# Two extra PSUM banks of a first layer: two one-bank tiles instead of the halves of a two-bank tile

## The chip, the core and the metric

The kernel runs on one core of a Trainium2 chip. A core has a matrix engine (TensorE, PE in the profile; its weight loads are shown apart as PEld), three engines for element-wise work (VectorE or DVE, ScalarE or ACT, GpSimd or POOL) and SyncE (SP), which here issues DMAs. POOL issues DMAs too. The engines run side by side, each through its own instructions in order, and wait for one another through semaphores. A matmul writes into PSUM, a small memory that is cut into banks; one bank holds 128 x 512 numbers of 32 bits. VectorE and ScalarE read it from there.

The metric is the device time of one execution in microseconds (us). Less is better.

## What is computed

Attention with two kinds of fixed mask, followed by a two-layer network with a leaky activation:

```python
def _attn_ref(q, k, v):                      # [8, 8, 576, 64] each
    stride = 32
    scores = (1 / sqrt(64)) * q @ k^T
    rel = pos[:, None] - pos[None, :]
    mask_local = (rel >= 0) & (rel < stride)                       # heads 0 to 3
    mask_strided = (rel >= 0) & (pos[None, :] % stride == pos[:, None] % stride)   # heads 4 to 7
    scores = where(mask, scores, -1e9)
    return softmax(scores) @ v

def _moe_ref(x, w_in, w_out, alpha):         # x [4608, 512], w_in [512, 2048], w_out [2048, 512]
    h = x @ w_in
    g = maximum(h, 0) + alpha * minimum(h, 0)
    return g @ w_out                         # [4608, 512]

x = attention output with its heads side by side: [8 * 576, 512]
```

## The kernel before

**Tiling.** The 4608 tokens are nine chunks of 512. Layer 1 of a chunk is 16 groups m = 0 to 15 of 128 hidden features each; a group is four matmuls of 128x512 (one for each 128 of the 512 input features, kk) that add up in one PSUM bank. ScalarE then writes the negative part to SBUF (`neg`, L646), and VectorE joins it with the bank to the activated group `gT[:, m]` (the function `fin` in `lin1_piece`, L649). Only after `fin` may the bank be written again. Layer 2 of chunk 0 is 16 pieces ("M" 0 to 15, `lin2_piece`, L664): four token tiles of four pieces, each piece four matmuls that read four groups of `gT` and a quarter of `wout`.

Attention goes batch by batch, in pairs of heads: a pair g is number g % 4 of batch g // 4, and pairs 2 and 3 of a batch are strided. Its steps are T (transposes of q and k, L255, with the tails t of the last 64 tokens, L273 and L278), S (scores, ScalarE's exponential and a mask, L421 to L443 from batch 2 on), P (attention times v, `pv_piece`, L469, with VectorE's division L478 and L480) and X (transposes of the result to xT, L488). P waits for the mask of the scores it reads. T is named by u, half a batch: T 3 q is the strided half of batch 1, T 4 of batch 2 the other half.

**Order.** Everything is kept in program order on each engine. For batch 0 and chunk 0 that order is written out as a list (`first`): loads, casts, attention of batch 0, and at its end the marker "B" and the first matmuls of groups 2, 1 and 0 ("L"), of which layer 1's loop does the last kk. Then the loop `for m in (2, 1, 0, *range(3, 16))` runs layer 1 of chunk 0 with no attention in between (`attn_n(0, 0)` does none). A second list runs layer 2 of chunk 0 mixed with attention of batch 1: M 0, M 1, M 2, M 4, M 3, then T 3 q, M 5, t 3, T 3 k, and so on. From chunk 1 on, layer 1 and layer 2 pieces alternate with attention steps of later batches, which come from a list `pieces`; the attention functions there also issue casts and loads to POOL and transposing DMAs (`transpose_d`, L137) to SyncE. A piece of g = 8 issues to POOL, in this order: its first mask (L436), the two copies of the strided v of batch 2 (L195, from the loaded tile `stv`), the next v load (L175) and, when the deferred exponentials are done, its second mask (L443).

**PSUM.** There are eight banks in three pools. `pspool` (tag "ps") has three slots of one bank that are given out in turn: transposes (`tp`, `tt`), outputs of P (`pv`), of X (`xp`) and, from batch 2 on, half of the scores (`sph`) use them. `phpool` has three banks hb0 to hb2, each a tile of its own. `pbpool` has a single tile of two banks (tag "sp"), which the scores use.

`hbank` (L84) gives out banks for layer 1, layer 2 and some of the scores, from a list `banks`, in the order of the list `turn` of indices: it takes the first one and puts it at the end. Up to "B" only hb0 and hb1 turn (hb2 is the target of matmuls on zeros, L815, that occupy TensorE at the start). At "B" `more_banks` (L875) takes the two-bank tile from `pbpool`, appends its two halves to `banks` as numbers 3 and 4, and sets `turn` so that groups 2, 1, 0, 3, 4 get hb2, hb0, hb1, half 0, half 1, and so on in that circle of five: m = 3, 8 and 13 use half 0 and m = 4, 9 and 14 use half 1. After layer 1 the numbers 3 and 4 leave `turn`. The framework places the tiles and derives the waits between engines from which instruction uses which tile.

Of the kernel before, what the change touches and what calls it, by code (L numbers as in the profile page):

```python
# [9 lines left out]
F32 = mybir.dt.float32  # L10
# [21 lines left out]
def kernel(  # L32
# [13 lines left out]
    B, H, S, D = q.shape  # L46
# [16 lines left out]
    pspool = ctx.enter_context(tc.tile_pool(name="ps", bufs=3, space=bass.MemoryType.PSUM))  # L63
    phpool = ctx.enter_context(tc.tile_pool(name="ph", bufs=1, space=bass.MemoryType.PSUM))
    pbpool = ctx.enter_context(tc.tile_pool(name="pb", bufs=1, space=bass.MemoryType.PSUM))
# [15 lines left out]
    banks = [phpool.tile([128, 512], F32, tag=f"hb{i}", name=f"hb{i}") for i in range(3)]  # L81
    turn, busy = [0, 1], []
# [534 lines left out]
    def lin1_mm(n, m, kks, first, last):  # L617
        if first:
            hcur[m] = hbank()
        hps = hcur[m]  # L620
        c0 = (512 * n) % RING
        parts = [(c0, 0, min(512, RING - c0))]
        if c0 + 512 > RING:
            parts.append((0, RING - c0, 512 - (RING - c0)))
        for kk in kks:
            for x, (src, dst, w) in enumerate(parts):
                keep(nc.tensor.matmul(  # L627
                    hps[:, dst : dst + w],
                    win16[:, kk, 128 * m : 128 * m + 128],
                    xT[:, kk, src : src + w],  # L630
                    start=(first and kk == kks[0] and x == 0),
                    stop=(last and kk == kks[-1] and x == len(parts) - 1),
                    skip_group_check=True,
                ))
        return hps

    def lin1_piece(n, m):
        if n not in gTs:
            gTs[n] = gpool.tile([128, 16, 512], F16, tag="gT", name="gT")
        if n == 0 and m < 3:  # L640
            hps = lin1_mm(n, m, (0,), False, True)
        else:
            hps = lin1_mm(n, m, (2, 0, 3, 1) if n == 1 else range(4), True, True)

        neg = npool.tile([128, 512], F32, tag="neg", name="neg")
        keep(nc.scalar.activation(neg, hps, AF.Relu, scale=-1.0))  # L646

        def fin():
            keep(nc.vector.scalar_tensor_tensor(  # L649
                gTs[n][:, m, :], neg, oma[:, m : m + 1], hps, op0=ALU.mult, op1=ALU.add))  # L650
        late.append(fin)
# [168 lines left out]
    def load_unit(b, strided, v_too=True):  # L820
# [3 lines left out]
        if v_too:  # L824
# [7 lines left out]
            name=nc.get_next_instruction_name(), act_func_set_id=6, ins=[], outs=[]  # L832
# [39 lines left out]
        for c, second in which:  # L872
            load_w(c, second)

    def more_banks():  # L875

        sp = pbpool.tile([128, 2, 512], F32, tag="sp", name="sp")
        banks.extend([sp[:, 0], sp[:, 1]])
        turn.insert(0, 2)
        turn.extend([3, 4])  # L880

    do = {
        "T": lambda u, nm: transpose_piece(u, nm),
        "t": lambda u: tails(u // 2, u, u % 2 == 1),
# [7 lines left out]
        "A": slope,  # L892
        "W": warm,
        "L": lambda m, hp: lin1_mm(0, m, (hp,), hp == 2, False),
        "B": more_banks,
    }

    first = [
# [22 lines left out]
    def attn_n(n, end):  # L921
        for _ in range(n):
            attn_step(end)
        if n == 0:
            attn_step(0)

    for m in (2, 1, 0, *range(3, 16)):
        lin1_piece(0, m)
        attn_n(0, 0)
    for z in (3, 4):  # L930
# [88 lines left out]
```

## Time and profile before

| | |
|---|---|
| time, median of 4 runs | 308.64 us (308.52 to 308.95) |
| time of the profiled execution | 308.6 us |
| its span, first to last instruction | 306.7 us |
| mean granted TensorE clock | 0.994 |
| TensorE busy | 295.0 us (96%), 2775 matmuls |
| VectorE, ScalarE, POOL busy | 222.1, 176.7, 168.4 us |
| chain that ended last, by engine | PE 85%, DMA 4%, DVE 4%, POOL 3% |

The span in forty slices of 7.67 us, busy share in tenths, and the granted clock:

```
PE   7997789999999999999999999999999999999995
DVE  5785638968853889588857886788668958955872
ACT  3753527577556776477647764776477236516630
POOL 8862288539769873877397719771836102101300
PEclk9997999999999999999999999999999999999999
```

How to read it: a 9 is a slice that is busy for 90% or more. Layer 1 of chunk 0 lies in slices three to six (19.5 to 41.3 us), layer 2 of chunk 0 from there to 64 us. Matmuls are pipelined and their ends are modelled, so a following matmul starts up to 0.15 us before the shown end of the one before. An entry in square brackets behind a line of the timeline is the idle time of the engine before it and what ended it. Where an instruction waits for several things, the view names the one that came last by its own account.

### The profile page before, as it was taken

The numbers are of one execution on the slowest core, as the hardware profiler recorded it, in microseconds if no ns is written. First come the engines' busy times: TensorE is split into PE (matmuls) and PEld (weight loads), VectorE is DVE, ScalarE is ACT, GpSimd is POOL, SyncE is SP. The second block draws the span as 40 slices with busy tenths as digits, with TensorE's granted clock in tenths as the row PEclk, the third lists the DMA queues.
The fourth block names the chain that finished last, engine by engine and source line by source line (L and its number), as shares of the span: only waits on it lengthen the run. The fifth ranks groups of instructions, "written<-read, shape, count | busy, mean of one in ns | idle before, by whom it ended". The sixth has DMA issues, their size and how long they took to land.

```text
span 306.7 us, 7027 instructions
## 1 busy us (share of the span) xinstructions
PE 295.0 (96%) x2775; PEld 191.8 (63%) x2775; DVE 222.1 (72%) x421; ACT 176.7 (58%) x330; POOL 168.4 (55%) x178
## 2 busy tenths in 40 slices
PE   7997789999999999999999999999999999999995
PEld 3562345654555458845888888448844874685484
DVE  5785638968853889588857886788668958955872
ACT  3753527577556776477647764776477236516630
POOL 8862288539769873877397719771836102101300
PEclk9997999999999999999999999999999999999999
DMA  7999997999799981999389938972821040012004
GB/s 226 191 205 207 205 223 200 144 174 204 207 153 209 218 106 16 148 302 117 41 141 295 116 35 126 209 83 37 183 82 22 0 142 18 2 66 72 2 0 139
DMA packets 81201, 40.38 MB, mean 132 GB/s; under 512 B 58624, under 2 KB 76304, under 8 KB 81168
## 3 DMA queue, kind: packets, MB, share of 16 engines
q0 software_dynamic: 41728, 17.38, 48.5%
q1 hardware_dynamic: 39168, 22.03, 30.8%
q10 hardware_dynamic: 272, 0.52, 0.6%
q8 instruction: 22, 0.36, 0.5%
q14 instruction: 11, 0.09, 0.1%
HBM read 38.01 MB, written 9.44 MB: 155 GB/s over the span
## 4 chain that ended last, share of the span: by engine, by line
PE 85%; DMA 4%; DVE 4%; POOL 3%; ACT 1%; issue 1%; ACTq 0%; POOLq 0%
PE hb L627 39%; PE hb L757 25%; PE hb L664 7%; PE pv L469 4%; DMA tl<-in_q_dram 2%; DMA ql<-in_q_dram 2%; PE tp L255 2%; PE sp L421 2%; PE sp L627 2%; DVE gT L649 2%; PE opl L757 1%; DVE gsum L709 1%; PE sph L421 1%; PE xp L488 1%; ACT neg L646 1%
## 5 line engine op out<-in xcount | busy, mean ns | idle before, releaser
L627 PE MATMUL hb<-xT,win 128*128 128x512 f16 (+1 forms) x616 | 129.1, 360 | 0.0
L649 DVE SCALAR_TENSOR_TENSOR gT<-neg,oma,hb 128x512 f16<-128x512 f32 x138 | 100.8, 744 | 36.4 <-ACT neg L646 29.9
L646 ACT ACTIVATE neg<-hb 128x512 f32<-128x512 f32 x138 | 82.2, 597 | 37.3 <-PE hb L627 36.7
L627 PEld LDWEIGHTS <-win 128*128 128x128 f16 x640 | 60.1, 98 | 60.6 <-issue 8.2
L436 POOL TENSOR_TENSOR et<-et,consts 128x576 f16<-128x576 f16 (+1 forms) x24 | 30.6, 1277 | 43.5 <-ACT et L434 43.4
L709 POOL TENSOR_TENSOR gsum<-gT 128x512 f16<-128x512 f16 x21 | 24.1, 1149 | 52.0 <-DVE gT L649 52.0
L757 PEld LDWEIGHTS <-gsum 128*128 128x128 f16 x448 | 41.6, 98 | 4.9 <-DVE gsum L709 0.2
L480 DVE TENSOR_TENSOR x<-pv,rc 96x384 f16<-96x384 f32 (+2 forms) x62 | 33.0, 532 | 2.1
L757 PEld LDWEIGHTS <-gT 128*128 128x128 f16 x336 | 31.5, 98 | 4.8
L443 POOL TENSOR_TENSOR et<-et,consts 128x576 f16<-128x576 f16 (+1 forms) x24 | 31.5, 1314 | 2.2 <-ACT et L440 2.2
L664 PE MATMUL hb<-wout,gT 128*128 128x512 f16 x128 | 31.9, 379 | 0.2 <-ACT osb L669 0.2
L469 PEld LDWEIGHTS <-et 72*128 72x128 f16 (+1 forms) x448 | 23.8, 98 | 10.5 <-DVE x16s L480 0.6
L769 ACT COPY o<-hb 128x512 f32<-128x512 f32 (+1 forms) x28 | 15.8, 565 | 24.1 <-PE hb L757 24.1
L757 PE MATMUL hb<-wout,gT 128*128 128x256 f16 x216 | 27.3, 273 | 0.0
L757 PE MATMUL hb<-wout,gsum 128*128 128x256 f16 x216 | 26.9, 273 | 0.0
L434 ACT ACTIVATE et<-sp 128x576 f16<-128x576 f32 (+1 forms) x24 | 15.5, 645 | 18.3 <-PE sp L421 16.7
L757 PE MATMUL hb<-wsum,gsum 128*128 128x256 f16 x216 | 26.0, 273 | 0.0
L772 DVE TENSOR_TENSOR o<-hb,o 128x512 f32<-128x512 f32 (+1 forms) x21 | 14.3, 679 | 14.7 <-PE hb L757 10.7
L478 DVE RECIPROCAL rc<-pv 72x6 f32<-72x6 f32 (+2 forms) x80 | 14.6, 182 | 10.2 <-PE pv L469 9.9
L440 ACT ACTIVATE et<-sph 128x288 f16<-128x288 f32 (+1 forms) x48 | 18.9, 409 | 0.0
L664 PEld LDWEIGHTS <-gT 128*128 128x128 f16 x128 | 11.0, 97 | 9.8 <-issue 0.2
L469 PE MATMUL pv<-vs,et 72*128 72x65 f16 x256 | 15.6, 194 | 0.3 <-DVE x16s L480 0.3
(107 smaller groups left out, 330.6 us busy)
## 6 DMA issues: line engine op xcount, KB each, us to landing
out_dram<-o SPq DMA_DIRECT2D x27, 256.0 KB, 4.0
kl<-in_k_dram SPq DMA_DIRECT2D x6, 512.0 KB, 7.7
ql<-in_q_dram SPq DMA_DIRECT2D x5, 512.0 KB, 7.2
stv<-in_v_dram POOLq DMA_DIRECT2D x8, 288.0 KB, 7.3
vl<-in_v_dram POOLq DMA_DIRECT2D x6, 384.0 KB, 8.2
win<-in_moe_w_in_dram POOLq DMA_DIRECT2D x4, 512.0 KB, 12.6
wout<-in_moe_w_out_dram POOLq DMA_DIRECT2D x4, 512.0 KB, 16.6
out_dram<-osb SPq DMA_DIRECT2D x8, 256.0 KB, 4.5
```

The source lines that it names most:

```text
L436: keep(nc.gpsimd.tensor_tensor(mv, mv, m, op=ALU.mult))
L440: keep(nc.scalar.activation(ev[:, n * y : n * y + n], sps[y][0:r, 0:n], AF.Exp, scale=SCALE))
L443: keep(nc.gpsimd.tensor_tensor(mv, mv, m, op=ALU.mult))
L469: keep(nc.tensor.matmul(pv[:, 65 * x : 65 * x + 65], et[0:r, c : c + 128], v16[0:r, 2 * P.pr + hh, t, :] if P.strided else v16[:, 6 * (2 * ...
L480: keep(nc.vector.tensor_tensor(P.x16[0:w, c0 : c0 + 64 * nb].rearrange("r (c e) -> r c e", e=64), pvv[:, :, 0:64], rc[0:w, 0:nb].unsqueeze ...
L627: keep(nc.tensor.matmul(hps[:, dst : dst + w], win16[:, kk, 128 * m : 128 * m + 128], xT[:, kk, src : src + w], start=(first and kk == kks ...
L646: keep(nc.scalar.activation(neg, hps, AF.Relu, scale=-1.0))
L649: keep(nc.vector.scalar_tensor_tensor(gTs[n][:, m, :], neg, oma[:, m : m + 1], hps, op0=ALU.mult, op1=ALU.add))
L664: keep(nc.tensor.matmul(ops, gTs[n][:, kf, 128 * mt : 128 * mt + 128], wout16[:, kf, :], start=(kf == 0), stop=(kf == 15)))
L709: keep(eng.tensor_tensor(o[:, k0:k1], x[:, k0:k1], y[:, k0:k1], op=op))
L757: keep(nc.tensor.matmul(dst, lhs[:, kf, 128 * mt : 128 * mt + 128], rhs[:, kf, :], start=(first and own and kf == 0), stop=(kf == 7), skip ...
L769: keep(nc.scalar.copy(o, x))
```

## The change

`more_banks` and its two-bank tile go. The marker "B" now only puts hb2 at the head of `turn`. In the loop of layer 1, ahead of groups 3 and 4, one tile of one bank each is taken from `pspool`, appended to `banks` as number 3 or 4, and its number is put at the head of `turn`. The circle of five is the same as before. No instruction is added or removed, and the two tiles go back to their pool when their last reader (the `fin` of m = 13 and of m = 14) is done.

```diff
-    def more_banks():
-
-        sp = pbpool.tile([128, 2, 512], F32, tag="sp", name="sp")
-        banks.extend([sp[:, 0], sp[:, 1]])
-        turn.insert(0, 2)
-        turn.extend([3, 4])
-
...
-        "B": more_banks,
+        "B": lambda: turn.insert(0, 2),
...
     for m in (2, 1, 0, *range(3, 16)):
+        if m in (3, 4):
+            banks.append(pspool.tile([128, 512], F32, tag="ps", name="hx"))
+            turn.insert(0, m)
         lin1_piece(0, m)
         attn_n(0, 0)
```

## The prediction

> **What bounds the kernel now.** I read the page first: TensorE is busy 295.0 of 306.7 us, so a gain must come from where it is idle or slow. Its row of forty slices is below 9 in the first fifth alone, and the granted clock is below 9 only in the fourth slice (23.0 to 30.7 us). That is layer 1 of chunk 0. So I asked the trace for the line of those matmuls in all, L627, and then for TensorE in order of time.
>
> ```profile
> its engine sat idle before it (us, times) until:
>   issue: 8.2, 11
>   DVE gT L649: 5.1, 3
> ```
>
> Line L627 waits for VectorE three times in the whole run, 5.1 us together ("issue" is the weight loads, which wait for nothing that counts). The timeline (start, length, instructions) says where:
>
> ```profile
> 22.80 1.03 PE L627 MATMUL sp<-xT,win 128*128 128x512 f16 x4
> 25.97 1.26 PE L627 MATMUL sp<-xT,win 128*128 128x512 f16 x4 [2.15 <-DVE gT L649]
> 27.03 4.24 PE L627 MATMUL hb<-xT,win 128*128 128x512 f16 x12
> 31.11 1.03 PE L627 MATMUL sp<-xT,win 128*128 128x512 f16 x4
> 33.60 1.02 PE L627 MATMUL sp<-xT,win 128*128 128x512 f16 x4 [1.47 <-DVE gT L649]
> 34.46 2.75 PE L627 MATMUL hb<-xT,win 128*128 128x512 f16 x12
> 37.05 1.03 PE L627 MATMUL sp<-xT,win 128*128 128x512 f16 x4
> 39.55 1.02 PE L627 MATMUL sp<-xT,win 128*128 128x512 f16 x4 [1.47 <-DVE gT L649]
> ```
>
> Banks are used in the order hb2, hb0, hb1, sp half 0, sp half 1. The second half waits each time. For what, VectorE's timeline shows:
>
> ```profile
> 25.18 0.74 DVE L649 SCALAR_TENSOR_TENSOR gT<-neg,oma,sp 128x512 f16<-128x512 f32 x1
> ...
> 32.80 0.75 DVE L649 SCALAR_TENSOR_TENSOR gT<-neg,oma,sp 128x512 f16<-128x512 f32 x1
> ```
>
> The first ends at 25.92 and half 1 starts at 25.97; the second ends at 33.55 and half 1 starts at 33.60. So half 1 waits until half 0, written just before it, has been read. The two share no element. No hb bank waits for its neighbour: being one tile is what ties them.
>
> The first wait costs more than itself. Windows of line L627:
>
> ```profile
> core 0: us, PE busy (x) PEld busy (x), PEclk, DMA share, GB/s
> 26.50:27.10 0.60, 0.60 (x4) 0.20 (x2) 0.60 1.24 205
> 27.60:28.00 0.40, 0.40 (x3) 0.12 (x2) 0.50 1.25 207
> 30.00:30.50 0.50, 0.50 (x4) 0.24 (x3) 0.97 1.23 203
> ```
>
> The clock is 0.60, then 0.50, and back at 30.0.
>
> **The sum in this stage.** A matmul of 128x512 takes 0.216 us in a row without waits (the chain of waits has 12 in 2.59 us), a group of four 0.864. From m = 3 (22.80) to the first matmul of layer 2 (41.27) there are 13 groups: 13 x 0.864 = 11.23, but 18.47 pass. The excess is 7.24: waits of 2.15 + 1.47 + 1.47 = 5.09; 0.15 for each that the modelled end of the matmul before covers, 0.45; and the slow clock, 0.6 x 0.40 + 2.9 x 0.50 = 1.7.
>
> [...] In the trace the slow stretch follows the 2.15 us wait within 0.6 us and lasts 3.4; the two 1.47 us waits have none behind them. I take the trace: all **7.24 us** go, and a new wait of about 2 us can bring 1.7 back.
>
> **What takes their place.** The new tiles come from the pool of three one-bank slots that transposes and attention outputs use. The two slots that m = 3 and m = 4 get held the outputs of P(0,1) and X(1), which VectorE has read by 21.5; TensorE wants them at 22.80 and 23.66. Cost nothing. Both stay taken until VectorE has finished m = 13 and m = 14, while layer 2's first transposes (T 3 q) want slots. These come behind M 3, which needs m = 15 finished, so that too is covered; without that cover they would wait up to one 0.60 us ACT and one 0.75 us DVE instruction. The order of banks and the number of instructions do not change. Waits that only name another instruction: below, a tenth of a us either way; I take nothing.
>
> Can the next engine keep up? Per group ACT needs 0.60 and VectorE 0.75 us, under 0.864. VectorE starts its first at 23.20 and is behind by four; m = 5, 6 and 7 want banks at 24.5, 25.4 and 26.3, read by 23.9, 24.6 and 25.2. The weights: win's four loads were issued at 7.80, 9.75, 11.14, 11.9 and took 11.6, 12.1, 13.2, 15.0, so m = 4, 8 and 12 have theirs at 21.9, 24.4, 26.9 and want them at 23.7, 27.1, 30.6. Layer 2 would begin at 34.03.
>
> **Layer 2, 7.2 us early.** From 20 to 58 us POOL waits for landings and then works through its casts; it waits for TensorE only at 62.04. These times stay. Each item that TensorE needs from there, moved 7.24 early:
> - wout's last two quarters land at 34.5 and 37.1 (18.1 + 16.4, 18.8 + 18.2); M 2 and M 3 want them at 35.8 and 37.5. Nothing.
> - T 3 q stands at 45.59, so 38.35; qs lands at 19.7 + 18.7 = 38.4. A tenth.
> - t 3 stands at 46.99, so 39.75; its tail lands at 27.1 + 13.2 = 40.35. **The lead falls to about 6.5.**
> - T 2 q, t 2, T 2 k, P(4,0), T 4 q, T 4 k: at 43.4, 45.6, 46.7, 51.8, 53.6, 56.7 with lead 6.5; casts and loads are done at 42.8, 45.1, 45.4, 50.1, 51.2, 53.7. Nothing.
>
> **Chunk 1.** It starts at 57.5 instead of 64.08, and here POOL's order bites:
>
> ```profile
> 68.09 1.27 POOL L436 TENSOR_TENSOR et<-et,consts 128x576 f16<-128x576 f16 x1 [4.62 <-ACT et L434]
> 69.32 2.01 POOL L195 COPY vs<-stv 72x1024 f16<-72x1024 f16 x2
> 71.28 0.82 POOL L175 DMA_DIRECT2D stv<-in_v_dram  x1
> 72.12 1.29 POOL L443 TENSOR_TENSOR et<-et,consts 128x576 f16<-128x576 f16 x1
> ```
>
> The second mask ends at 73.41 and P(8,1), which reads it, starts on TensorE at 73.83. With the lead the first mask is at 61.6, but the copies read a load issued at 55.09 that took 9.5 us to land: 64.6. From there copies 2.0, DMA issue 0.8, mask 1.3: end 68.74. P(8,1) stood 0.4 behind its mask; of that I count 0.3 as room (the rest, an estimate, as the start after a release). TensorE waits from 67.3 to 68.8, **1.5 us**, and the lead is 73.41 - 68.74 + 0.3 = **5.0**.
>
> Does that load land at 64.6 again? SyncE's two transposes of q and k (issued 64.02 and 67.06, landed 6.7 and 6.3 later) sit behind the last store of layer 2, and would now start when their source lands, 53.6 + 6.9 = 60.5, beside the end of this load. The nearest rows: vl loads took 6.4 us without these transposes (issued 51.2) and 7.7 with them (62.0), so at most 1.3 later. [...] I take the rows, 0.4 between 0 and 1.3, since only the last part of the load meets them.
>
> Behind it: the k transpose lands near 63.6 + 6.3 = 69.9, wanted by the score at 75.86 - 4.6 = 71.3; the next k load (issue 71.33 + 7.3 = 78.6, where POOL's cast starts at 78.69) moves with the transposes, 3.4 us, and lets P(10,0), which has 2.1 us of slack, start 5.5 early. Neither is tighter than 4.6. From 64 us on TensorE is busy in every slice and waits 0.3 us in all, so the lead reaches the end.
>
> **Forecast: 7.2 - 0.7 - 1.5 - 0.4 = 4.6 us.** The profiled execution took 308.6 us (span 306.7, 1.9 around it), as the median 308.64: **304.0 us**. Its own range is 302.9 to 305.0.
>
> **Rivals.**
> - *The loads are early* (10%). A later v load (71.28) landed 5.8 us after issue. Then the copies wait for nothing, mask 2 ends at 66.9, and if the source of the transposes comes 1 us early too, P(10,0) lets the lead stand at 6.5: 302.1. With the v load alone P(10,0) would set 5.5, which is 303.1 and in the forecast's own range. Against: 9.5 is this very load, and nothing ahead of it changes.
> - *The clock falls again* (22%). The wait at P(8,1) reaches 2 us, and half rate takes 1.7 again: lead 2.6 to 3, 306.0. For: 1.5 plus the 0.4 is at the edge. Against: 1.47 did not do it.
> - *The lead is lost at 64 us* (4%). The chain of waits gives 6.92 us from 57.03 to a tail load that ends at the matmul at 63.97; if it held, the stage would end where it does: 308.6. Against: the tile read there is loaded at 45.3 and 45.9, landing 5.4 and 5.0 later; VectorE's copy that frees the slot ends at 63.7 and explains the wait.
> - *Slower* (7%). The v load is held up by the transposes beyond 14.5 us, past 69.6 us, where the lead is used up; with half rate behind so long a wait, past 67.9. Landing at 70.5 gives 308.6 + 0.9 + 1.7 = 311.2. For: loads issued at 20 to 22 took 18.7 and 17.5. Against: those stood behind the eight weight loads.
>
> The forecast has 56%. The range is 302.0 to 306.6: it takes in the first two rivals and leaves out the last two and the tails. 0.2%, 0.6 us, is what a measurement of this kernel tells from no change. Faster 0.89, within 0.04, slower 0.07.
>
> **What would show it.** No wait of line L627 for VectorE between 22 and 42 us, clock 1.00 there, layer 2 at 34.0; a wait of half a us at t 3; chunk 1 at 57.5; one wait of 1.5 to 2 us at P(8,1) near 67 us for POOL; none after. Wrong if the second new bank still waits for the first, if layer 2 stalls for loads beyond 1 us, or if the clock falls elsewhere.

## The result and the profile after

The changed kernel is no faster than the one before: ratio of times 1.0018 [0.9998, 1.0038], where the forecast of 304.0 us was 0.985. The ratio leaves out executions more than 1.5% above the fastest of the same kernel, which are 18 of 33 of the changed kernel and 3 of 54 of the kernel before; over all of them the medians are 310.98 us (305.86 to 315.13) and 307.85. No gain is to be seen in either count. The profiled execution took 309.59 us with a span of 307.8, against 308.6 and 306.7 before.

Up to 68 us the trace does what the sum said. TensorE's timeline of the changed kernel (start, length, engine, line, instructions; in brackets the idle time before and what ended it):

```profile
23.05 1.89 PE L627 MATMUL hx<-xT,win 128*128 128x512 f16 x8
24.77 2.75 PE L627 MATMUL hb<-xT,win 128*128 128x512 f16 x12
27.36 1.89 PE L627 MATMUL hx<-xT,win 128*128 128x512 f16 x8
...
33.41 1.03 PE L627 MATMUL hb<-xT,win 128*128 128x512 f16 x4
34.27 4.48 PE L664 MATMUL hb<-wout,gT 128*128 128x512 f16 x20
...
57.10 2.75 PE L627 MATMUL hb<-xT,win 128*128 128x512 f16 x12
...
68.77 0.36 PE L469 MATMUL pv<-vl,et 128*128 128x65 f16 x6 [1.75 <-POOL et L443]
68.96 1.89 PE L627 MATMUL hb<-xT,win 128*128 128x512 f16 x8
```

The two new banks (`hx`) are written in one go, eight matmuls without a wait. From m = 3 (23.05) to layer 2 (34.27) 11.22 us pass. Layer 2 begins 7.00 us early (41.27 before), chunk 1 6.98 early (64.08 before), and behind P(8,1)'s wait the lead is still 5.06 us (73.83 before). Then it is lost. The table of TensorE's waits (total us, times, longest) and the timeline go on:

```profile
PE sp L421 <- DMA kT<-ksd: 3.5, 1, 3.5
PE pv L469 <- POOL et L443: 1.8, 1, 1.8
```

```profile
74.40 0.42 PE L421 MATMUL sp<-qT,kT 64*128 64x72 f16 x8 [3.54 <-DMA kT<-ksd]
...
74.99 3.60 PE L627 MATMUL hb<-xT,win 128*128 128x512 f16 x8
...
81.16 1.89 PE L664 MATMUL hb<-wout,gT 128*128 128x512 f16 x8
```

The score S(10), the first that reads the q and k which SyncE transposes by DMA, waits 3.54 us for k. It started at 75.86 before, so 1.46 us of lead are left. Behind it eight matmuls take 3.60 us instead of 1.89, and layer 2 of chunk 1 begins 6.76 us after the score (74.40 to 81.16), where the kernel before needed 4.20 (75.86 to 80.06). That is 2.56 us more: 1.46 - 2.56 = -1.10, and the spans differ by just that. The windows show why (stretch, its length, busy us of PE, PEld, DVE, ACT and POOL with instructions, granted clock, DMA share, GB/s):

```profile
core 0: us, PE busy (x) PEld busy (x) DVE busy (x) ACT busy (x) POOL busy (x), PEclk, DMA share, GB/s
68.00:70.00 2.00, 1.23 (x11) 0.68 (x12) 1.17 (x3) 0.00 (x0) 2.00 (x3) 1.00 1.56 56
72.00:74.00 2.00, 0.00 (x0) 0.00 (x0) 0.27 (x1) 0.00 (x0) 0.00 (x0) 0.74 1.91 159
74.00:76.00 2.00, 1.60 (x19) 0.93 (x20) 0.00 (x0) 0.94 (x2) 0.00 (x0) 0.50 1.08 305
76.00:78.00 2.00, 2.00 (x7) 0.65 (x5) 0.45 (x1) 0.89 (x2) 1.04 (x1) 0.50 1.05 386
78.00:80.00 2.00, 2.00 (x12) 0.98 (x11) 1.04 (x3) 0.60 (x1) 2.00 (x2) 0.55 1.17 373
```

The clock falls to 0.50 during the wait and stays there until almost 80 us. In the row of forty slices the low clock has moved with it, from the fourth slice (layer 1 of chunk 0) to the tenth and eleventh (69 to 85 us):

```profile
PEclk9999999997899999999999999999999999999999
```

So the old stall and its half clock are gone, and a stall and a half clock of much the same size stand 50 us later. What that stall waits for, in SyncE's timeline and the view of the tile kT, before (first) and after:

```profile
64.02 2.93 SPq L137 DMA_TRANSPOSE qT<-qsd  x1
67.06 3.44 SPq L137 DMA_TRANSPOSE kT<-ksd  x1
...
DMA to landing us min/median/max: 6.3/6.3/6.3
```

```profile
60.25 2.40 SPq L137 DMA_TRANSPOSE qT<-qsd  x1
62.93 4.37 SPq L137 DMA_TRANSPOSE kT<-ksd  x1
...
DMA to landing us min/median/max: 11.4/11.4/11.4
```

The k transpose is issued 4.1 us earlier (62.93 for 67.06) and takes 11.4 us from issue to landing instead of 6.3: it lands at 74.35, later than the 73.3 of before. The q transpose takes 10.6 instead of 6.7. A third transfer is stretched too: the load of batch 3's v (`vl`, issued by POOL behind the tails, the last part of `load_unit(3, False)` ahead of chunk 1). It waited 3.76 us for TensorE before, so the lead let it move up by 3.9. POOL's timeline and the view of vl, before (first) and after:

```profile
62.04 1.44 POOL L183 DMA_DIRECT2D vl<-in_v_dram  x1 [3.76 <-PE xp L488]
...
DMA to landing us min/median/max: 7.7/7.7/7.7
```

```profile
58.17 1.44 POOL L183 DMA_DIRECT2D vl<-in_v_dram  x1 [0.21 <-PE hb L627]
...
DMA to landing us min/median/max: 16.3/16.3/16.3
```

It took 7.7 us before and takes 16.3 now.

### The profile page after: what moved, and what is told of

It reads as the page before. It is cut to its first block, busy times and chain, and to the rows that moved or that the text cites. A ratio compares the mean times of both kernels' runs of the same rounds, so it can differ in the third digit from the quotient of the medians.

```text
span 307.8 us, 7027 instructions
## 1 busy us (share of the span) xinstructions
PE 295.1 (96%) x2775; PEld 191.7 (62%) x2775; DVE 221.9 (72%) x421; ACT 176.9 (57%) x330; POOL 168.1 (55%) x178
## 4 chain that ended last, share of the span: by engine, by line
PE 84%; DVE 6%; DMA 6%; ACT 1%; issue 1%; POOL 1%; ACTq 0%; POOLq 0%
PE hb L627 36%; PE hb L757 25%; PE hb L664 8%; PE pv L469 4%; DMA kT<-ksd 4%; PE tp L255 2%; DMA ql<-in_q_dram 2%; PE hx L627 2%; PE sp L421 2%; DVE x L480 2%; PE opl L757 1%; DVE gsum L709 1%; PE xp L488 1%; PE sph L421 1%; DVE rc L478 1%
## 5 line engine op out<-in xcount | busy, mean ns | idle before, releaser
L627 PE MATMUL hb<-xT,win 128*128 128x512 f16 (+1 forms) x616 | 129.8, 361 | 0.0
L627 PEld LDWEIGHTS <-win 128*128 128x128 f16 x640 | 60.2, 98 | 55.1 <-issue 2.4
L772 DVE TENSOR_TENSOR o<-hb,o 128x512 f32<-128x512 f32 (+1 forms) x21 | 14.3, 679 | 14.7 <-PE hb L757 10.9
```

The source lines that it names most:

```text
L627: keep(nc.tensor.matmul(hps[:, dst : dst + w], win16[:, kk, 128 * m : 128 * m + 128], xT[:, kk, src : src + w], start=(first and kk == kks ...
```

## The experiments

Two causes were open at first. In the kernel before, the pair of transposes began (64.02) when the strided loads of batch 2 (`stv`, landed at 64.6, and the tails behind it, the last at 57.63 + 8.1 = 65.7) were nearly in. Those loads wait for POOL alone and have not moved; the pair and the v load of batch 3 have, by 3.8 and 3.9 us, and both now run beside them. Either the strided loads or the v load could be what stretches the pair. The first four kernels take away the one or the other, put the transposes later, and make one of the edits in the kernel before.

**The v load of batch 3 later** (the changed kernel otherwise):

```diff
-    load_unit(3, False)
+    load_unit(3, False, False)
...
             second["on"] = i >= 16
+            if n == 1 and i == 16:
+                load_v(3, False)
```

> The changed kernel with the v load of batch 3 (issued at 58.2 us there, 16.3 us to landing) moved behind layer 1 of chunk 1. Theory A (the two transposes are slow because several POOL loads are still in flight beside them: k source, v, tails and this one): the q transpose lands in 8 to 9.5 us instead of 10.6, the k transpose at 72 to 73 us instead of 74.35, the wait of the score falls from 3.5 to about 1.5 us and the time is 1 to 2 us under the changed kernel. Rival B (this one load does it): the k transpose lands as in the kernel before, 6.3 us after issue, near 69.5 us; the wait goes, the clock does not fall after it, and the time is 4 us or more under the changed kernel. Rival C (the q and k loads behind the transposes on SyncE's own queue do it): the landing stays within 0.5 us of 74.35 and so does the time.

Measured: 0.9857 [0.9831, 0.9882]. The transposes start at 60.78 and 63.16, within 0.5 us of the changed kernel's, and take 7.9 and 6.6 us. SyncE's timeline and the view of kT, with TensorE's waits from 20 to 90 us of this kernel:

```profile
60.78 1.68 SPq L137 DMA_TRANSPOSE qT<-qsd  x1
63.16 3.25 SPq L137 DMA_TRANSPOSE kT<-ksd  x1
...
DMA to landing us min/median/max: 6.6/6.6/6.6
```

```profile
PE pv L469 <- POOL et L443: 1.9, 1, 1.9
PE tp L255 <- DVE rc L478: 0.2, 1, 0.2
PE hb L664 <- ACT osb L669: 0.2, 1, 0.2
```

k lands at 69.8, the wait at the score is gone, the clock stays at 1.00, and the lead at layer 2 of chunk 1 is 4.86 us (75.20 for 80.06). One load moved away brings back what the forecast had promised: 0.0143 x 308.6 = 4.4 us. The q and k loads of batch 3 still follow on SyncE's queue (from 66.52), so they alone do not stretch the pair to 10.6 and 11.4 us.

**The transposes held until chunk 1's m = 4 is done**, by a tiny copy on SyncE that reads that group:

```diff
-                    if g % 4 == 3 and DX <= c + 1 < B:
+                    if g % 4 == 3 and DX < c + 1 < B:
                         transpose_d()
...
-    load_unit(3, False)
+    load_tail(3, False)
+    load_v(3, False)
+    gate = cpool.tile([1, 64], F16, name="gate")
...
+            if n == 1 and i == 6:
+                keep(nc.sync.dma_start(gate, gTs[1][0:1, 4, 0:64]))
+                transpose_d()
+                load_qk(3, False, "q")
+                load_qk(3, False, "k")
```

> The changed kernel with the two transposes held back until VectorE has finished m = 4 of chunk 1 (near 63.6 us) by a 128-byte copy on SyncE's queue ahead of them; the q and k loads of batch 3 stay behind them. Theory A: begun 3.4 us later they land no later, q at 6.5 to 8 us and k at 6 to 8 us after issue, the k transpose at 73 to 74.5 us: the earlier start was worth nothing. Rival B says the same only if the v load of batch 3 has landed by then; it lands later than 66 us, so B expects k no earlier than 76 us. Rival C: latencies of 10.6 and 11.4 us again, k at 77 to 78 us, and the time 3 us over the changed kernel.

Measured: 1.004 [1.0015, 1.0064]. This run does not test what it was made for: in its trace chunk 1 begins only at 61.80, 4.7 us later than in the changed kernel, and the copy came at 68.19. VectorE's masks at 51 us took 3.67 us instead of 1.55, and TensorE's clock was 0.50 from about 56.2 to 59.6 us (for both see the last section). The transposes then start at 68.92 and 71.25, take 6.7 and 5.5 us, and k lands at 76.8, so that the score waits 3.2 us. What it does show is that a pair that starts when the v load (issued 60.0, 10.1 us) is near its end is short.

**The strided loads of batch 2 ahead of its casts**, in the changed kernel and in the kernel before:

```diff
-        ("P", 6, 1), ("t", 2), ("C", 1, "k", 1, "pool"), ("I", load_tail, 2, False), ("M", 9),
+        ("P", 6, 1), ("t", 2), ("C", 1, "k", 1, "pool"), ("I", load_d, 2), ("I", load_v, 2, True), ("I", load_tail, 2, False), ("M", 9),
...
-        ("I", cast_l, 2, "q"), ("I", load_v, 2, False), ("I", cast_l, 2, "k"), ("I", load_d, 2),
-        ("I", load_v, 2, True), ("K", 7), ("X", 6), ("P", 7, 0), ("S", 4), ("P", 7, 1), ("M", 11),
+        ("I", cast_l, 2, "q"), ("I", load_v, 2, False), ("I", cast_l, 2, "k"),
+        ("K", 7), ("X", 6), ("P", 7, 0), ("S", 4), ("P", 7, 1), ("M", 11),
```

> The changed kernel with the loads that the transposes and the copies of v read (q, k and v of batch 2's strided heads) issued ahead of the casts, near 45 us instead of 53 to 55. Theory A: all have landed by 55 us, the transposes start behind the last store of layer 2 at 56.5 to 57 with only tails and one v load beside them, the k transpose is there before the score wants it (69.3 us), the wait at P(8,1) goes too, the clock stays at 1.00, and the lead of 6.5 us over the kernel before reaches the end: 6 us less than before, ratio 0.980. Rival D (the late transposes are a matter of their own and of the v load of batch 3): the waits at P(8,1) go but the score still waits 2 us or more; 2 to 3 us less than before.

> The kernel before with the same loads moved ahead of the casts. TensorE waited for none of them there, so both theories expect the time of the kernel before, ratio 0.998 to 1.002. If moving the loads is worth something by itself (less crowding later), it shows here, and what e3 gains has to be read less this.

Measured: 0.9895 [0.9879, 0.9912] in the changed kernel, 0.9986 [0.9969, 1.0003] in the kernel before. In the changed kernel `stv` is out of the way, but the transposes start 3 us earlier as well (57.13 and 59.31), beside the tails and a v load issued at 58.75 that took 11.1, and still take 8.9 and 10.3 us. The gain is that k, begun so early, lands at 69.6, in time, and that P(8,1) does not wait. It also shows that the strided loads are not needed for a long k transpose: the last of them landed at 58.2, before k was issued. Part is given back at the tails of batch 2, which now stand behind these loads: TensorE waits 2.0 us for them in layer 2 (L278).

Four further kernels followed. **More beside the transposes**, the q and k loads of batch 3 ahead of them on SyncE:

```diff
-        ("P", 5, 1), ("X", 4), ("M", 15), ("X", 7), ("X", 5), ("G",),
+        ("P", 5, 1), ("X", 4), ("M", 15), ("X", 7), ("X", 5),
+        ("I", load_qk, 3, False, "q"), ("I", load_qk, 3, False, "k"), ("G",),
     ])
...
-    load_unit(3, False)
+    load_tail(3, False)
+    load_v(3, False)
```

> The changed kernel with the q and k loads of batch 3 issued on SyncE ahead of the two transposes (near 57 us) instead of behind them (67.4 us); the v load of batch 3 stays where it is. Theory B1 (the v load and the k transpose beside each other are enough): the k transpose is still late, 10 us or more behind its issue and past 73 us; the score still waits 2.5 us or more and the time is within 1 us of the changed kernel. Theory B2 (it takes the q and k loads beside these two): the k transpose lands 6 to 8 us after issue, before 72 us; the wait falls under 1.5 us and the time is 3 us under the changed kernel. Either way POOL's wait of 5.5 us for the q load goes.

Measured: 1.0144 [1.0097, 1.0192], worse than expected. The transposes take 12.7 and 12.9 us, the v load 21.5, k lands at 78.6, and the score waits 6.8 us. The clock is 0.50 behind it. More transfers beside the pair go with longer ones, and the time follows.

**The wait filled**, with fourteen matmuls on zeros ahead of the score, so that only the clock differs:

```diff
             acc -= cnt
+            if n == 1 and i == 11:
+                wz = pspool.tile([128, 512], F32, tag="ps", name="wz")
+                for _ in range(14):
+                    keep(nc.tensor.matmul(wz, wrm[:, 0:128], wrm, start=True, stop=True))
             attn_n(cnt, ab)
```

> The changed kernel with 14 matmuls on zeros (3.0 us, into a free slot, no one reads them) on TensorE just ahead of the score that waits 3.5 us for the k transpose. If the half clock behind that wait is what takes the rest of the lead: the clock stays at 1.00 from 70 to 80 us, the wait for the transpose shrinks to 0.5 us, everything behind comes 2 to 2.6 us earlier than in the changed kernel, ratio 0.993 to 0.996. If the clock is not part of it, the time is that of the changed kernel.

Measured: 1.0019 [0.9989, 1.0049], a miss: no gain to be seen. TensorE's timeline of this kernel:

```profile
70.35 3.19 PE L985 MATMUL wz<-gsum 128*128 128x512 f16 x14
...
75.29 0.30 PE L421 MATMUL sp<-qT,kT 64*128 64x72 f16 x8 [1.75 <-DMA kT<-ksd]
...
79.49 0.81 PE L664 MATMUL hb<-wout,gT 128*128 128x512 f16 x3
```

The mechanism is as expected: the wait is cut to 1.75 us, the clock stays at 1.00, and from the score to layer 2 4.20 us pass, as in the kernel before. But the score comes at 75.29, 0.9 us later than in the trace of the changed kernel, since k landed at 75.2 (11.8 us). Layer 2 of chunk 1 begins at 79.49, 1.67 us earlier than there.

**Both moves together**: the v load of batch 3 late, and the strided loads of batch 2 ahead of the casts but behind the tails:

```diff
-        ("P", 6, 1), ("t", 2), ("C", 1, "k", 1, "pool"), ("I", load_tail, 2, False), ("M", 9),
+        ("P", 6, 1), ("t", 2), ("C", 1, "k", 1, "pool"), ("I", load_tail, 2, False), ("I", load_d, 2), ("I", load_v, 2, True), ("M", 9),
```

> The changed kernel with the v load of batch 3 behind layer 1 of chunk 1 and with the strided q, k and v loads of batch 2 right behind the tail's, ahead of the casts. If the waits of the first two experiments are all that stands in the way: no wait of TensorE above 0.5 us behind layer 1 of chunk 0 save that at t 3, the clock at 1.00 throughout, the lead of 6.5 us is kept: ratio 0.979, 301.8 to 302.5 us where the kernel before takes 308.5. If moving loads only moves the crowding, a new wait of 1 to 2 us shows for another landing and the ratio is 0.984 to 0.988.

Measured: 0.9822 [0.9791, 0.9852], a little above the 0.979 that was expected. The transposes take 3.9 and 4.1 us and TensorE does not wait for them. In this trace VectorE's masks took 3.77 us near 51 us (see the last section), with waits of 0.92 and 0.79 us behind them, and chunk 1 starts at 59.31.

**The v load of batch 3 late in the kernel before**:

> The kernel before with the v load of batch 3 behind layer 1 of chunk 1. TensorE waited for no transpose there, so moving this load alone is worth nothing: ratio 0.998 to 1.002, and the gain of the first experiment belongs to the two together. If the late v load helps by itself, 1 us or more less than before.

Measured: 0.9988 [0.9967, 1.001], with transposes of 3.8 and 4.2 us. There k had time to spare, so a shorter transpose is worth nothing. The gain of the first experiment is therefore not a gain of its edit as such; it exists only with the lead.

The last four kernels are the changed kernel and the filled wait again side by side, then the v load alone beside the transposes (the loads moved as in "both moves", the v load left where the change has it), and both moves again.

> The changed kernel once more, unaltered, beside the next run, so that the two are compared on one chip. Theory: the transposes again land 10 us or more after their issue, the score waits 3 us or more, the clock falls to 0.50 behind it; 307 to 311 us.

> The fill of 14 matmuls on zeros ahead of the waiting score again, beside the changed kernel. In the first trace of it the stretch from that score to layer 2 of chunk 1 took 4.20 us, as in the kernel before, where it took 6.76 in the changed kernel. If that clock loss is in most executions of the changed kernel, the median here is 2 to 2.6 us under that of the run beside it and the spread of the runs is narrower; if it is only in the one that was traced, the medians agree within 0.6 us.

Measured: 1.0008 [0.9983, 1.0033] for the changed kernel and 0.9982 [0.9964, 0.9999] for the filled wait. The first repeats its trace: transposes of 11.0 and 11.3 us beside a v load of 14.3, a wait of 2.75 us at the score, clock 0.50 behind it, 5.87 us from the score to layer 2. The filled one has 4.20 us there again, and 20 of its 22 executions have a mean granted clock of 0.997 or more, against 3 of 22. The difference in time, 0.26% or 0.8 us, lies between the two expectations, and the intervals overlap; over all 22 executions of each the medians are 309.15 and 307.50, 1.65 us apart. That the clock falls behind this wait is shown; how much filling the wait pays is not settled.

> The changed kernel with the strided q, k and v loads of batch 2 ahead of the casts (behind the tail's), and the v load of batch 3 left where it is, so that beside the two transposes there are only that load and 128 KB of tails. If each POOL load in flight beside them adds its part (none: 3.9 and 4.1 us to landing; v of batch 2 and tails: 7.9 and 6.6; all: 10.6 and 11.4): 7 to 9 us for q and 7 to 10 for k, the k transpose there by 69 us, no wait of the score above 1 us, ratio 0.982 to 0.988. If the v load of batch 3 alone does all the harm: 10 us or more for both, the score waits 1 to 3 us, ratio 0.990 or more.

Measured: 0.9905 [0.9879, 0.9932]. With the strided loads out of the way and the v load (58.1, 12.7 us) beside it, the q transpose takes 7.2 us, the k transpose 11.2. SyncE's timeline and the view of kT, then the wait:

```profile
57.22 2.03 SPq L137 DMA_TRANSPOSE qT<-qsd  x1
59.37 3.49 SPq L137 DMA_TRANSPOSE kT<-ksd  x1
...
DMA to landing us min/median/max: 11.2/11.2/11.2
```

```profile
PE sp L421 <- DMA kT<-ksd: 1.5, 1, 1.5
```

Although k starts 3.6 us earlier than in the changed kernel, the score waits 1.54 us for it. Neither expectation is met whole: q is as short as in the first, k and the wait are as long as in the second. The strided loads had landed by 58.1, so beside k there were the v load and the tails. (Its trace has another wait of 4.9 us between 91 and 110 us which no other trace shows; only the part up to 80 us is read here.)

> The version with both loads moved once more, for a second trace and a tighter interval. The first trace had a stretch near 51 to 54 us in which VectorE's four masks took 3.77 us instead of 1.55 beside POOL's casts. If that is a matter of how the two happen to meet, this trace may show 1.55 again, chunk 1 then starts at 57.1 us as in the changed kernel, the k transpose lands within 5 us of its issue, no wait above 1 us: 301.4 to 302.7 us, ratio 0.979 to 0.983. If the moved loads cause it, the masks take over 3 us again and chunk 1 starts near 59.5 us.

Measured: 0.9819 [0.977, 0.9869], profiled at 301.8 us. This is the best version; in both its runs the interval lies below 0.99. TensorE's timeline:

```profile
69.19 0.30 PE L421 MATMUL sp<-qT,kT 64*128 64x72 f16 x8
...
73.39 0.81 PE L664 MATMUL hb<-wout,gT 128*128 128x512 f16 x3
```

The masks took 1.55 us again and chunk 1 starts at 57.41. The k transpose took 5.8 us, a little over the 5 expected; the score does not wait, the lead is 6.67 us at both places (75.86 - 69.19 and 80.06 - 73.39), and the span of 300.0 is 6.7 us shorter than that of before.

Put together, the time from issue to landing of the two transposes, by how long the last of POOL's tails was still in flight when q began (its landing less q's issue) and by the v load of batch 3:

| kernel | tails in flight, us | v load issued | q, us | k, us | v, us |
|---|---|---|---|---|---|
| before, v late | 1.0 | much later | 3.8 | 4.2 | |
| both moves | 2.6 | much later | 3.9 | 4.1 | |
| v late | 5.6 | much later | 7.9 | 6.6 | |
| both moves, again | 6.9 | much later | 7.1 | 5.8 | |
| transposes held | landed before q | 8.9 ahead of q | 6.7 | 5.5 | 10.1 |
| before, loads first | 0.8 | 2.0 ahead of q | 6.3 | 5.2 | 7.3 |
| before | 1.7 | 2.0 ahead of q | 6.7 | 6.3 | 7.7 |
| v load alone | 7.0 | 0.9 behind q | 7.2 | 11.2 | 12.7 |
| loads first | 7.6 | 1.6 behind q | 8.9 | 10.3 | 11.1 |
| changed | 6.6 | 2.1 ahead of q | 10.6 | 11.4 | 16.3 |
| changed, again | 7.4 | with q | 11.0 | 11.3 | 14.3 |
| wait filled | 7.0 | 1.8 ahead of q | 10.8 | 11.8 | 13.6 |
| wait filled, again | 7.1 | 1.6 ahead of q | 10.8 | 11.6 | 15.3 |
| q and k loads ahead | 8.9 | 1.8 ahead of q | 12.7 | 12.9 | 21.5 |

Without the v load k takes at most 6.6 us, with the tails in flight for up to 6.9. With it k takes 5.2 to 6.3 when POOL's other loads are in or nearly in, and over 10 in all seven traces where the pair begins 6.6 us or more ahead of the last landing of a tail. Neither alone goes with the 11 us; the two together do.

## Why the prediction was wrong

- **The 7.24 us of the stage: right.** 11.22 us for the thirteen groups (11.23 in the sum), no wait of L627 for VectorE, clock 1.00. The new tiles cost nothing and layer 2 begins at 34.27 (34.03). The lead of 7.00 is 0.24 short because m = 3 itself starts at 23.05 instead of 22.80. (TensorE's row of forty slices is below 9 in the last slice too, not in the first fifth alone; nothing rests on it.)
- **Its 1.7 us of half clock: right for the traced execution, not for every one.** The trace of the kernel before with the loads first has the same wait of 2.15 us, and the clock stays at 1.00 behind it. TensorE's timeline of that kernel:

```profile
26.14 1.02 PE L627 MATMUL sp<-xT,win 128*128 128x512 f16 x4 [2.15 <-DVE gT L649]
...
39.75 3.62 PE L664 MATMUL hb<-wout,gT 128*128 128x512 f16 x16
```

From m = 3 (22.96) to layer 2 (39.75) 16.79 us pass there, 1.68 less than the 18.47 of the trace that the prediction read: there the stage is worth about 5.6 us, not 7.24. Of the 49 executions of the kernel before that were timed beside the repeat of the changed kernel, 28 have a mean clock of 0.997 or more. The four times known to the prediction, 308.52 to 308.95 us, were high ones: the median of all 54 is 307.85, so about 0.8 us of the forecast was luck of the sample.
- **0.7 lost at t 3: not seen.** The tails landed earlier in this execution, and t 3 starts at 39.99, 7.00 early.
- **1.5 + 0.4 at P(8,1): right.** The `stv` load lands at 54.78 + 9.8 = 64.6, the copies start at 64.62, the wait is 1.75 us and the lead behind it 5.06 (5.0). For this load the rows gave 0 to 1.3 us and the sum took 0.4: it did not land later at all (64.6 in both traces).
- **The failing step: "the k transpose lands near 63.6 + 6.3 = 69.9".** It was issued 0.7 us earlier than that and landed at 74.35, because it took 11.4 us. The 6.3 was taken from the trace of before as if it belonged to the transpose. It belonged to its neighbours: there the tails were in flight for only 1.7 us beside the pair and the v load landed at 69.7, 2.7 us after k's issue. Now the tails are beside the pair for 6.6 us and the v load for all of it (to 74.5). The prediction moved the pair and saw that it would meet the `stv` load, but asked only what the pair does to that load and not the reverse. The v load it never listed among what the lead moves, though it had read that POOL waits for TensorE at 62.04, which is just this load. "Neither is tighter than 4.6" rested on both. That this is the step is shown by the first experiment: without the v load the same transpose takes 6.6 us, lands at 69.8, and 4.4 us of the 4.6 come out.
- **Its price had two terms.** 3.54 us of wait took the lead from 5.0 to 1.46, and the half clock behind it took 2.56 more. That a wait of about 2 us brings the slow clock was in the prediction, as a rival at P(8,1) with 22%. There it stayed away (1.75 us, clock 1.00); it came one step further on and cost more than the 1.7 counted, because the clock was low for about 6.8 us there, against 3.4 in the trace of before.
- **The range.** The forecast and the first two rivals let the lead reach the end at 2.6 us or more, the upper end of 306.6 at 2.0. A transfer that is slower because something else starts with it was counted only as the 7% case of a held-up strided v load, at the wrong transfer.

What stays open is how the transfers stretch each other. It does not look like a mere division of a full rate: from 68 to 70 us 56 GB/s pass at a DMA share of 1.56 (the time that packets took, against that of the 16 engines), from 74 to 80 us 305 to 386 at 1.05 to 1.17. Nor is the part of the tails settled: they were never taken away alone, and the traces in which they are long beside the pair are also those in which the pair begins early.

## What to carry to other kernels

A stall removed early in a kernel brings forward every transfer that is issued behind it, while those that wait for something else stay (here the pair came 3.8 us earlier and the v load 3.9, while `stv` landed at 64.6 as before): list which transfers become neighbours, and price each with the duration that it has beside such neighbours (here 11.4 us for k), not with the one in the old trace (6.3). Where a gain disappears, look for the first wait behind it whose releaser is a transfer that starts earlier and lands no earlier. If that transfer has a neighbour nobody needs yet, move the neighbour back with the change; here one load made the difference between nothing and 1.4%.

## What the hardware showed that was not expected

The same DMA transpose took from 3.8 to 12.9 us, and the same v load from 7.3 to 21.5, with different transfers in flight beside them (the table of the experiments).

The clock fell to 0.50 around every wait of 2.75 us or more (2.75, 3.17, 3.54, 4.93 and 6.77) and stayed at 1.00 behind each single wait of 1.36 to 1.99 us. At 2.15 us it did both: half clock in the traces of before and of before with v late, none in that of before with the loads first. And two short waits can do it: with the transposes held, the clock fell at 56.2 us behind waits of 0.92 and 0.79 us that stand close together, while the same two waits in the first trace of both moves left it at 1.00. So the edge near 2 us that the prediction took from one wait is not an edge, and the length of a wait alone does not decide; what does is not shown. Read from windows of half a microsecond, each low stretch ahead of the last matmul lasted either about 3.4 us (five of them) or about 6.8 (three), so by these traces a fall costs at half rate about 1.7 or up to 3.4 us, less what falls into the wait itself (estimates).

The same code has two faces at 51 us, where VectorE's masks and POOL's casts meet. First VectorE's timeline in the first trace of both moves, then VectorE's and POOL's in the second:

```profile
50.71 3.77 DVE L329 TENSOR_TENSOR et<-et,consts 128x576 f16<-128x576 f16 x4
```

```profile
50.90 1.55 DVE L329 TENSOR_TENSOR et<-et,consts 128x576 f16<-128x576 f16 x4
...
50.69 2.66 POOL L195 CAST ql<-ql 128x1024 f16<-128x1024 f32 x1
```

In the first the masks take 3.77 us and the cast beside them, begun at 50.27, 1.04; in the second the masks take 1.55 and the cast 2.66. So the masks are 2.22 us longer in the first, the cast 1.62 us longer in the second. In both the cast begins first by these records, by 0.44 us in the first and 0.21 in the second (times of POOL are rough); what makes the one or the other longer is not shown. In the run with the held transposes the masks took 2.1 us more, and the half clock from 56.2 us for about 3.4 us took about 1.7 (an estimate): together 3.8 of the 4.7 us by which chunk 1 began late.
